# A gated recurrence and highway layer on one core: smaller first units, one shared set of work buffers and a new order of operations

## The chip, the cores and the metric

The kernel runs on one core of a Trainium2 chip. The metric is device time in microseconds; lower is better. Three runs of the kernel before took 207.35, 207.47 and 208.76 us (median 207.47).

## The reference

`x` and `f_logit` are 4 sequences of 6336 tokens with 256 features in fp32. A gated running state goes along each sequence, and a highway layer with two 256x256 matrices follows.

```
sig = 1 / (1 + exp(-f_logit))
f = lower_bound + (1 - lower_bound) * sig;   i = 1 - f
h[t] = f[t] * h[t-1] + i[t] * x[t]           # per sequence and feature, h starts at 0
H = relu(h @ w_h);   T = sigmoid(h @ w_t + b_t)
out = T * H + (1 - T) * h                    # 25344 x 256, fp32
```

## The kernel before, in words

The 25344 tokens are 198 blocks of 128. They are cut into **units** (`parts`): one unit is one tuple, with one or two subtiles of up to 8 blocks, so that (8, 8) is a unit of 2048 tokens. Units are worked in order, since the state runs on from one to the next. The features are two halves of 128 partitions (`h` or `m` = 0, 1). Each step of a unit is one letter in the string `order`, and the program issues the steps exactly as that string lists them; every engine then works its own steps in that order and waits where an input or a buffer isn't ready. The token `s10.0` is the step `s` of unit 10, half 0; the number after a colon names the buffer or the PSUM banks; a `v` at the end puts the step on VectorE (DVE) where it could run on another engine.

The steps, with their engines:

- `l`, `x`: loads of `f_logit` and `x` for one subtile (SP's queue; 1 MB for 8 blocks). `w`: store of a result (SP's queue too).
- `u`: u = sigmoid(-logit), fp16 (ScalarE, ACT).
- `b`, `B`: products bv = u * x, half of a subtile or all of it (GpSimd, POOL; with `v` on DVE).
- `i`, `p`: TensorE (PE) transposes of u and of bv into PSUM. `f`: f = 1 + ncc * u (ACT, with `v` DVE).
- `s`: the scan y = f * y + bv over one half of a unit (DVE). It reads the transposed bv of all the unit's subtiles.
- `z`, `g`: the two matmuls on y. `t`: sigmoid of z (ACT). `d`: max of g and the scaled y (DVE).
- `e`, `E`: the gate d = d * t, for one half or both (POOL, with `v` DVE).
- `o`: matmuls that bring y and d back to token order. `c`: copy out of PSUM (ACT, with `v` DVE).
- `k`: matmuls on zeros, whose result nobody uses.

`WI`, `WH`, `WT`, `dg`, `pc`, `cc` prepare weights and per-feature scalars once. Two rules of the code matter later. The helper `shared` records the last `b` or `e` that DVE did, and makes the next `b` or `e` on POOL wait until that one has ended. And each kind of tile has numbered buffers of its own (`u0`, `bv0`, `f0`, ...), so that a step waits for the last reader of its buffer.

Of the kernel before, what the change touches and what calls it, by code (L numbers as in the profile page):

```python
# [19 lines left out]
def kernel(  # L20
# [454 lines left out]
```

## Time and profile before

| | |
|---|---|
| timed runs | 207.35, 207.47, 208.76 us |
| span of the profiled execution, first to last instruction | 205.8 us (its own device time isn't listed apart; the median of the timed runs lies 1.7 us above the span) |
| instructions | 4646 |
| busy: PE, DVE, ACT, POOL | 194.8, 192.4, 190.7, 173.8 us |
| moved by DMA | 78.67 MB, mean 382 GB/s |
| granted TensorE clock | 0.998 |

A PE that is busy isn't necessarily at its peak, since the ends of matmuls are modelled. DVE and ACT durations are recorded, with successive instructions overlapping a little. In a list by shape, "128x1024" is 128 partitions by 1024 elements of one partition. Idle time is booked to what ended it.

### The profile page before, as it was taken

The page shows a single profiled execution, that of the slowest core. Times are in us where ns is not written, and L with a number is a line of the kernel's source. Part 1 is how long each engine was busy: PE and PEld are TensorE (multiplying, and loading weights), DVE is VectorE, ACT ScalarE, POOL GpSimd, SP SyncE. Part 2 cuts the span into 40 slices and gives each one's busy share as a digit, 9 for nine tenths or more (in the row PEclk, how much of TensorE's full clock was granted, in tenths as well). Part 3 has the DMA queues.
Part 4 walks back from the last instruction along what each step waited for, and adds up shares of the span by engine and source line. Part 5 has one row for each costly group of instructions (what it writes and reads, how often), then busy time and mean ns, then how long its engine had stood idle before and what let it go on. Part 6 is the DMA issues. An engine that isn't in the chain of part 4 may idle for free.

```text
span 205.8 us, 4646 instructions
## 1 busy us (share of the span) xinstructions
PE 194.8 (95%) x1850; PEld 135.7 (66%) x1850; DVE 192.4 (93%) x147; ACT 190.7 (93%) x182; POOL 173.8 (84%) x85
## 2 busy tenths in 40 slices
PE   7989999969989999999999999999999999999992
PEld 2555775746765747757757858657757868777671
DVE  0679999999999999999999999999999999999992
ACT  5197999999999999999999999999999999999992
POOL 3634696999999999979999869999899788999760
PEclk9999999999999999999999999999999999999999
DMA  6999999999999999999999999999999999853766
GB/s 191 375 427 419 417 420 419 414 413 426 416 426 427 414 422 410 432 408 427 426 408 426 427 412 425 419 422 427 414 411 407 334 411 382 344 212 140 277 225 234
DMA packets 16700, 78.67 MB, mean 382 GB/s; under 512 B 1828, under 2 KB 2344, under 8 KB 10792
## 3 DMA queue, kind: packets, MB, share of 16 engines
q1 hardware_dynamic: 16672, 78.39, 93.9%
q8 instruction: 14, 0.23, 0.4%
q14 instruction: 6, 0.05, 0.1%
q10 hardware_dynamic: 8, 0.00, 0.0%
HBM read 52.43 MB, written 25.95 MB: 381 GB/s over the span
## 4 chain that ended last, share of the span: by engine, by line
PE 56%; DVE 24%; ACT 7%; issue 5%; DMA 5%; SPq 0%; DVEq 0%; ACTq 0%
PE psum L344 17%; DVE y L331 15%; PE psum L149 13%; DVE d L374 7%; PE psum L407 7%; PE psum L408 7%; PE psum L322 6%; PE psum L297 5%; ACT f L312 4%; DMA x<-in_x_dram 4%; ACT t L367 2%; DMA l<-in_f_logit_dram 1%; ACT u L273 1%; PE psum L250 1%; ACT o L427 1%
## 5 line engine op out<-in xcount | busy, mean ns | idle before, releaser
L288 POOL TENSOR_TENSOR bv<-u,x 128x1024 bf16<-128x1024 f16 (+2 forms) x39 | 101.4, 2615 | 20.0 <-DVE d L388 10.9
L331 DVE TENSOR_TENSOR_SCAN y<-f,y,psum 128x1024 bf16<-128x1024 f16 (+6 forms) x40 | 103.7, 2612 | 0.5 <-PE psum L407 0.4
L344 PE MATMUL psum<-y,w_sb 128*128 128x512 bf16 (+1 forms) x240 | 79.6, 368 | 4.2 <-ACT f L312 1.9
L388 POOL TENSOR_TENSOR d<-d,t 128x1024 bf16<-128x1024 bf16 (+3 forms) x33 | 71.5, 2180 | 4.6 <-ACT o L427 1.3
L374 DVE SCALAR_TENSOR_TENSOR d<-y,ncc,psum 128x1024 bf16<-128x1024 bf16 (+2 forms) x60 | 62.7, 1084 | 1.1 <-PE psum L344 0.4
L149 PE MATMUL psum<-y,w_sb 128*128 128x512 bf16 x168 | 63.6, 379 | 0.0
L367 ACT ACTIVATE t<-psum,bt 128x1024 bf16<-128x1024 f32 (+2 forms) x60 | 57.4, 988 | 0.9 <-PE psum L344 0.5
L273 ACT ACTIVATE u<-l 128x2048 f16<-128x2048 f32 (+2 forms) x28 | 48.1, 1744 | 6.5 <-DMA l<-in_f_logit_dram 6.5
L312 ACT ACTIVATE f<-psum,ncc 128x1024 f16<-128x1024 f16 (+3 forms) x38 | 50.3, 1344 | 1.2 <-PE psum L297 1.2
L407 PE MATMUL psum<-diag,y 128*128 128x128 f16 x396 | 49.7, 219 | 0.2
L408 PE MATMUL psum<-ident_b,d 128*128 128x128 bf16 x396 | 49.7, 219 | 0.0
L408 PEld LDWEIGHTS <-d 128*128 128x128 bf16 x396 | 43.5, 112 | 3.8 <-DVE d L388 0.4
L427 ACT COPY o<-psum 128x1024 f32<-128x1024 f32 (+1 forms) x46 | 44.2, 997 | 1.6 <-ACT f L312 0.6
L407 PEld LDWEIGHTS <-y 128*128 128x128 bf16 x396 | 43.6, 112 | 2.7
L344 PEld LDWEIGHTS <-w_sb 128*128 128x128 f16 x240 | 23.0, 98 | 20.1 <-issue 0.8
L322 PE MATMUL psum<-ident_f,bv 128*128 128x128 f32 x198 | 29.4, 275 | 0.8 <-ACT f L312 0.7
L149 PEld LDWEIGHTS <-w_sb 128*128 128x128 f16 x168 | 16.4, 97 | 20.2 <-issue 5.9
L297 PE MATMUL psum<-ident_h,u 128*128 128x128 f16 x396 | 28.8, 221 | 0.8 <-DVE y L331 0.4
L297 PEld LDWEIGHTS <-u 128*128 128x128 f16 x396 | 25.1, 99 | 5.7 <-issue 1.2
L322 PEld LDWEIGHTS psum<-ident_f,bv 128*128 128x128 f32 x198 | 22.4, 141 | 5.8 <-ACT f L312 1.4
L388 DVE TENSOR_TENSOR d<-d,t 128x1024 bf16<-128x1024 bf16 (+3 forms) x20 | 11.3, 596 | 0.1
L149 PE MATMUL psum<-zeros 128*128 128x512 bf16 x39 | 10.6, 398 | 0.0
(34 smaller groups left out, 43.1 us busy)
## 6 DMA issues: line engine op xcount, KB each, us to landing
l<-in_f_logit_dram SPq DMA_DIRECT2D x23, 1024.0 KB, 13.6
x<-in_x_dram SPq DMA_DIRECT2D x23, 1024.0 KB, 14.2
out_dram<-o SPq DMA_DIRECT2D x43, 512.0 KB, 8.0
out_dram<-x SPq DMA_DIRECT2D x7, 256.0 KB, 2.0
out_dram<-o SPq DMA_DIRECT2D x6, 256.0 KB, 9.3
l<-in_f_logit_dram SPq DMA_DIRECT2D x2, 512.0 KB, 6.5
x<-in_x_dram SPq DMA_DIRECT2D x2, 512.0 KB, 7.3
l<-in_f_logit_dram SPq DMA_DIRECT2D x3, 256.0 KB, 2.8
```

The source lines that it names most:

```text
L149: return pe.add_instruction(mybir.InstMatmult(name=nc.get_next_instruction_name(), start_tensor_calc=start, stop_tensor_calc=stop, tile_si ...
L288: shared(pin(e.tensor_mul(st[n]["bv", s][:, a:c].rearrange("p k d j -> p k j d"), st[n]["u", s][:, 2 * a:2 * c].rearrange("p (k j) d -> p ...
L297: pin(nc.tensor.transpose(uT[:, j * P:(j + 1) * P], st[n]["u", s][:, j, h * P:(h + 1) * P], ident_h))
L312: pin(nc.scalar.activation(to, of, AF.Identity, scale=ncc[:, h:h + 1], bias=1.0))
L322: pin(nc.tensor.transpose(words[:, k:k + g * (P - 1) + 1:g], pair, ident_f))
L331: pin(nc.vector.tensor_tensor_scan(y[:, c:e], st[n]["f", h][:, c:e], data, 0.0 if fresh else carry[h], op0=ALU.mult, op1=ALU.add))
L344: pin(nc.tensor.matmul(p.part(a, e), w, data, start=ki == 0, stop=ki == NH - 1))
L367: pin(nc.scalar.activation(half(n, q, "t", m), z, AF.Sigmoid, bias=bt[:, m:m + 1]))
L374: pin(nc.vector.scalar_tensor_tensor(half(n, q, "d", m), y, ncc[:, m:m + 1], g, op0=ALU.mult, op1=ALU.max))
L388: shared(pin(e.tensor_mul(d, d, t)), not eng)
L407: pin(nc.tensor.matmul(o, st[n]["y", h][:, whole], diag[:, h], start=True, stop=False))
L408: pin(nc.tensor.matmul(o, half(n, q, "d", h)[:, cols], ident_b, start=False, stop=True))
```

## The change

1. `parts` begins (1,), (1,), (2,), (4,) in place of (2,), (2,), (4,): the same first 8 blocks in four units in place of three, 22 units in all. From the fourth (8,) on everything is cut as before, under a number that is higher by one.
2. `lower_bound` and `moe_b_t` go to tiles of their own and are transposed apart (`pb`, `pc`); `bt` is copied by ACT (`cbv`).
3. `u`, `bv`, `f`, `y`, `t`, `d` and the results `o` take their buffers from one set, `work0` to `work28`; `l` and `x` from another, `large0` to `large9`. For units of at most 1024 tokens the two halves of `f`, and of `y`, lie in one buffer (`halves`).
4. `order` is written anew. Counted over the whole program:

| step and width (elements of one partition) | engine | before | after |
|---|---|---|---|
| products `b` 2048 / 1024 / 512 / 256 | DVE | 0 / 1 / 1 / 0 | 7 / 0 / 0 / 1 |
| products `b` 2048 / 1024 / 512 / 256 | POOL | 12 / 21 / 6 / 0 | 15 / 4 / 2 / 1 |
| gate `e` 2048 / 1024 / 512 / 256 / 128 | DVE | 1 / 11 / 3 / 5 / 0 | 9 / 6 / 2 / 0 / 0 |
| gate `e` 2048 / 1024 / 512 / 256 / 128 | POOL | 5 / 20 / 7 / 1 / 0 | 6 / 9 / 5 / 3 / 2 |
| `f` 1024 / 512 / 256 / 128 | DVE | 1 / 1 / 2 / 0 | 2 / 0 / 0 / 3 |
| copies out 1024 / 512 / 256 | DVE | 2 / 2 / 1 | 2 / 0 / 1 |
| weight scaling 256 | DVE / ACT | 2 / 2 | 4 / 0 |
| matmuls on zeros from `k` | PE | 49 | 23 |

Scans and `d` stay on DVE, with the same total of elements.

The core of the diff, with two lines of the old and the new `order` (the first of each):

```
-    parts = [(2,), (2,), (4,), (8,), (8,), (8,), (8,), (8, 8), ...
+    parts = [(1,), (1,), (2,), (4,), (8,), (8,), (8,), (8,), (8, 8), ...
-k*4:0 l1.0:0 u1.0:0 i1.0.0:0 i1.0.1:1 l0.0:1 x0.0:0 x1.0:1 u0.0:1 b0.0.0:0 pc:2 wh i0.0.0:3 i0.0.1:4 WI k*1:5 cc
+x0.0:0 l2.0:1 pb:0 pc:1 cc l0.0:2 u0.0:0 b0.0.0v:1 l1.0:3 u1.0:2 k*1:6 i0.0.0:7 i1.0.0:6 u2.0:3 i2.0.1:5 f1.0v:4
+    def work(dtype, name, slot):
+        return pool.tile([P, 2 * NB * P], dtype, tag=f"work{slot}", name=name)
+    def large(name, slot):
+        return pool.tile([P, NB, D], FP32, tag=f"large{slot}", name=name)
-    prm = sb([2 * NH, P], FP32, "prm")
-    pin(nc.scalar.dma_start(prm[:NH], lower_bound.rearrange("(h p) -> h p", p=P)))
-    pin(nc.scalar.dma_start(prm[NH:], moe_b_t.rearrange("(h p) -> h p", p=P)))
+    raw_lb = sb([NH, P], FP32, "raw_lb")
+    raw_bt = sb([NH, P], FP32, "raw_bt")
+    pin(nc.scalar.dma_start(raw_lb, lower_bound.rearrange("(h p) -> h p", p=P)))
+    pin(nc.scalar.dma_start(raw_bt, moe_b_t.rearrange("(h p) -> h p", p=P)))
...
-            st[n]["bv", s] = sb([P, NB // 2, D, 2], BF16, "bv", slot)
+            st[n]["bv", s] = work(BF16, "bv", slot)
...
+    def halves(n, name, dtype, h, slot):
+        N = tokens(n)
+        if N > NB * P:
+            st[n][name, h] = work(dtype, name, slot)[:, :N]
+        elif (name, 0) not in st[n]:
+            both = work(dtype, name, slot)
+            st[n][name, 0], st[n][name, 1] = both[:, :N], both[:, N:2 * N]
+        return st[n][name, h]
```

Three places show how the new order stands on the engines.

**The first loads on SP's queue**, before (`l` and `x` of units 1, 0, 2, 3, 4, ...; 512 elements are two blocks, `w_raw` the two weight matrices):

```order
L261 DMA l<-in_f_logit_dram 128x512 x2
L261 DMA x<-in_x_dram 128x512 x2
L208 DMA w_raw<-in_moe_w_h_dram 128x2x256
L261 DMA l<-in_f_logit_dram 128x1024
L205 DMA w_raw<-in_moe_w_t_dram 128x2x256
L261 DMA x<-in_x_dram 128x1024
L261 DMA l<-in_f_logit_dram 128x2048
```

and of the change:

```order
L278 DMA x<-in_x_dram 128x256
L278 DMA l<-in_f_logit_dram 128x512
L278 DMA l<-in_f_logit_dram 128x256 x2
L278 DMA x<-in_x_dram 128x256
L216 DMA w_raw<-in_moe_w_h_dram 128x2x256
L213 DMA w_raw<-in_moe_w_t_dram 128x2x256
L278 DMA x<-in_x_dram 128x512
L278 DMA l<-in_f_logit_dram 128x1024
L278 DMA x<-in_x_dram 128x1024
L278 DMA l<-in_f_logit_dram 128x2048
```

Ahead of the first 1 MB load (128x2048) stand the same bytes as before, 8 blocks of `l`, 8 of `x` and the two matrices, 2.5 MB in all, in smaller pieces and another order.

**DVE in the middle, around the scans of unit 9 before** (`y_1002` and `y_1060` are its two halves, `d_966` the gate of unit 8, the other rows `d` steps of units 7 to 9):

```order
L374 SCALAR_TENSOR_TENSOR d_966<-y_895,ncc_92,psum_61 128x1024
L374 SCALAR_TENSOR_TENSOR d_820<-y_742,ncc_92,psum_61 128x1024
L331 SCALAR_TENSOR_TENSOR y_1002<-f_905,y_895,psum_61 128x2048
L331 SCALAR_TENSOR_TENSOR y_1060<-f_876,y_853,psum_61 128x2048
L388 TENSOR_TENSOR d_966<-d_966,t_1062 128x2048
L374 SCALAR_TENSOR_TENSOR d_1146<-y_853,ncc_92,psum_61 128x1024
```

The same tokens are unit 10 in the change. On DVE (`bv_981` is `B10.0v`, the products of unit 10's first subtile; `y_993` and `y_1048` its scans; `bv_1037` is `B11.1v`; `d_794` and `d_956` the gates `E8.1v` and `E9.1v`):

```order
L310 TENSOR_TENSOR bv_981<-u_784,x_775 128x4x2x256
L364 SCALAR_TENSOR_TENSOR y_993<-f_864,y_895,psum_61 128x2048
L421 TENSOR_TENSOR d_794<-d_794,t_811 128x2048
L310 TENSOR_TENSOR bv_1037<-u_950,x_912 128x4x2x256
L364 SCALAR_TENSOR_TENSOR y_1048<-f_888,y_827,psum_61 128x2048
L421 TENSOR_TENSOR d_956<-d_956,t_999 128x2048
L407 SCALAR_TENSOR_TENSOR d_1123<-y_895,ncc_93,psum_61 128x1024
```

and on POOL beside it (`d_620` is `E7.0`, `bv_983` is `B10.1`, the products of unit 10's second subtile, `d_800` is `E8.0`, `bv_1189` is `B11.0`):

```order
L421 TENSOR_TENSOR d_620<-d_620,t_655 128x2048
L310 TENSOR_TENSOR bv_983<-u_788,x_804 128x4x2x256
L421 TENSOR_TENSOR d_800<-d_800,t_906 128x2048
L310 TENSOR_TENSOR bv_1189<-u_929,x_1035 128x4x2x256
L421 TENSOR_TENSOR d_1123<-d_1123,t_1030 128x1024 x2
```

Products of one unit are now split between the engines: those of the first subtile stand on DVE right ahead of the scan `y_993`, those of the second on POOL behind them, by the rule of `shared`.

**Near the end, DVE of the change** (`y_2302` are scans of unit 18, `y_2399` of 19, `y_2554` of 20; `d_2100` is the gate `E15.0v`, `d_2424` first two `d` steps and then the gate `E18.1v`):

```order
L421 TENSOR_TENSOR d_2100<-d_2100,t_2135 128x2048
L364 SCALAR_TENSOR_TENSOR y_2302<-f_2051,y_2215,psum_61 128x1024
L407 SCALAR_TENSOR_TENSOR d_2361<-y_2215,ncc_93,psum_61 128x1024 x2
L407 SCALAR_TENSOR_TENSOR d_2385<-y_2302,ncc_93,psum_61 128x512
L364 SCALAR_TENSOR_TENSOR y_2399<-f_2290,y_2302,psum_61 128x1024
L407 SCALAR_TENSOR_TENSOR d_2424<-y_2302,ncc_93,psum_61 128x512 x2
L407 SCALAR_TENSOR_TENSOR d_2385<-y_2302,ncc_93,psum_61 128x512
L364 SCALAR_TENSOR_TENSOR y_2399<-f_2290,y_2302,psum_61 128x1024
L421 TENSOR_TENSOR d_2424<-d_2424,t_2456 128x1024
L364 SCALAR_TENSOR_TENSOR y_2554<-f_2466,y_2399,psum_61 128x512 x2
```

and POOL beside it (`B18.0`, `B19.0`, the gates `E16.0` and `E17.0`, `B20.0`, `b21.0.0`):

```order
L310 TENSOR_TENSOR bv_2292<-u_1924,x_1951 128x4x2x256
L310 TENSOR_TENSOR bv_2363<-u_2193,x_2196 128x4x2x256
L421 TENSOR_TENSOR d_2202<-d_2202,t_2224 128x2048
L421 TENSOR_TENSOR d_2361<-d_2361,t_2350 128x2048
L310 TENSOR_TENSOR bv_2397<-u_2374,x_2049 128x2x2x256
L310 TENSOR_TENSOR bv_2472<-u_2431,x_908 128x2x256
```

`bv_2292` stands ahead of DVE's gate `E15.0v`. Between that gate and `E18.1v` POOL now has five whole steps, from `bv_2363` to `bv_2472`; the scans `y_2399` need the first of them, the scans `y_2554` the fourth, `bv_2397`.

More of the change, by code (lines that the diff above doesn't have):

```diff
@@ L317, in do_p @@
             st[n]["bT", h] = Banks(slot, BF16)
+        if units[n][1][s] == 1:
+            pin(nc.tensor.transpose(st[n]["bT", h].one(s)[:, :P], st[n]["bv", s][:, h * P:(h + 1) * P], ident_b))
+            return
         words = st[n]["bT", h].one(s).bitcast(FP32)
```

173 lines of the change are left out of this document (90 added, 83 removed).

## The prediction

> **What bounds the kernel now.** I read the busy times first, then the stages, then the groups of instructions by shape.
>
> ```profile
> PE 194.8 (95%) x1850; PEld 135.7 (66%) x1850; DVE 192.4 (93%) x147; ACT 190.7 (93%) x182; POOL 173.8 (84%) x85
> ```
>
> Four engines are above 80% of a span of 205.8 us, so the average singles out none. The stages do (window, then PE, PEld, DVE, ACT, POOL busy, granted clock, DMA share, GB/s):
>
> ```profile
> 0.00:10.00 10.00, 8.81 (x35) 4.17 (x36) 3.77 (x12) 3.43 (x5) 4.77 (x15) 1.00 0.79 281
> 10.00:25.00 15.00, 14.14 (x109) 8.91 (x107) 12.63 (x19) 13.28 (x19) 6.50 (x4) 1.00 1.01 420
> 25.00:100.00 75.00, 70.55 (x685) 49.81 (x684) 74.30 (x42) 74.06 (x58) 71.60 (x27) 1.00 1.02 419
> 100.00:200.00 100.00, 99.23 (x1005) 71.35 (x1003) 99.70 (x71) 98.06 (x100) 90.90 (x41) 1.00 0.92 368
> 200.00:206.00 6.00, 2.10 (x27) 1.42 (x24) 2.03 (x6) 1.86 (x4) 0.00 (x0) 0.92 0.59 219
> ```
>
> From 25 to 200 us DVE works 174.0 of 175 us. Its idle time is 6.2 + 2.4 = 8.6 us before 25 us and 3.8 us from 200 to the end at 205.8. Is that busy time work, or stretched by waiting? The shapes answer (total busy, mean ns of one, idle before):
>
> ```profile
> L374 DVE SCALAR_TENSOR_TENSOR d<-y,ncc,psum 128x1024 bf16<-128x1024 bf16 x42 | 51.6, 1271 | 0.6 <-issue 0.2
> L288 POOL TENSOR_TENSOR bv<-u,x 128x2048 bf16<-128x2048 f16 x12 | 49.5, 4132 | 3.9 <-DVE d L388 3.9
> L288 POOL TENSOR_TENSOR bv<-u,x 128x1024 bf16<-128x1024 f16 x21 | 45.1, 2161 | 9.7 <-DVE d L388 7.0 <-ACT t L367 2.1 <-ACT u L273 0.6
> L388 POOL TENSOR_TENSOR d<-d,t 128x1024 bf16<-128x1024 bf16 x20 | 42.5, 2137 | 2.3 <-ACT o L427 1.3 <-DVE d L388 1.0
> L331 DVE TENSOR_TENSOR_SCAN y<-f,y,psum 128x1024 bf16<-128x1024 f16 x18 | 41.5, 2331 | 0.4 <-PE psum L407 0.4
> L331 DVE TENSOR_TENSOR_SCAN y<-f,y,psum 128x2048 bf16<-128x2048 f16 x8 | 35.5, 4466 | 0.0
> L388 POOL TENSOR_TENSOR d<-d,t 128x2048 bf16<-128x2048 bf16 x5 | 20.4, 4083 | 0.1
> L388 DVE TENSOR_TENSOR d<-d,t 128x1024 bf16<-128x1024 bf16 x11 | 7.6, 719 | 0.0
> L374 DVE SCALAR_TENSOR_TENSOR d<-y,ncc,psum 128x256 bf16<-128x256 bf16 x6 | 2.6, 470 | 0.0
> L331 DVE TENSOR_TENSOR_SCAN y<-f,y,psum 128x256 bf16<-128x256 f16 x4 | 3.0, 738 | 0.0
> L388 DVE TENSOR_TENSOR d<-d,t 128x256 bf16<-128x256 bf16 x5 | 1.4, 294 | 0.0
> L288 DVE TENSOR_TENSOR bv<-u,x 128x1024 bf16<-128x1024 f16 x1 | 1.3, 1318 | 0.0
> L310 DVE TENSOR_SCALAR f<-psum,ncc 128x1024 f16<-128x1024 f16 x1 | 1.3, 1271 | 0.0
> L388 DVE TENSOR_TENSOR d<-d,t 128x512 bf16<-128x512 bf16 x3 | 1.3, 448 | 0.1
> L388 DVE TENSOR_TENSOR d<-d,t 128x2048 bf16<-128x2048 bf16 x1 | 1.2, 1200 | 0.0
> L236 DVE TENSOR_SCALAR w_sb<-w_raw,cc 128x256 f16<-128x256 f32 x2 | 0.8, 444 | 0.0
> L288 DVE TENSOR_TENSOR bv<-u,x 128x512 bf16<-128x512 f16 x1 | 0.7, 745 | 1.5 <-DMA x<-in_x_dram 1.5
> L425 DVE COPY o<-psum 128x512 f32<-128x512 f32 x1 | 0.7, 667 | 0.0
> ```
>
> A scan of 2048 elements takes 4466 ns and one of 1024 takes 2331, a constant 2.08 ns per element plus 0.2 us; one of 256 (738) lies on the same line. There is no room for hidden waits. **DVE's own work paces the kernel** from 25 us on, ACT is 1.9 us behind it, and POOL has slack.
>
> **The work that moves to DVE.** The step from 512 to 1024 elements of a product costs 1318 - 745 = 573 ns, so 2048 elements cost 1318 + 2 x 573 = 2464 ns.
>
> - Products: 7 x 2.46 = 17.2 us more, one of 256 (745 - 287 = 458 ns) 0.5 more, less 1.32 and 0.75: +15.6.
> - Gates: now 9 x 1.200 + 6 x 0.719 + 2 x 0.448 = 16.0; before 1.2 + 11 x 0.719 + 3 x 0.448 + 5 x 0.294 = 11.9: +4.1.
> - Small edits together: one more `f` of 1024 (1.27) and three of 128 (0.34 each, extrapolated) for 2.0 us of old ones, +0.3; two copies of 512 fewer, -1.3; weight scaling, +0.9; 8 scans and 8 `d` at the start in place of 6 each (six of 256 become four of 256 and four of 128, by the rows of 256 about 0.47 and 0.34 for 128), +0.9; the copy of `bt` gone, -0.1. Sum +0.7.
>
> That is 20.4 us in 7 more instructions. Successive instructions overlap: 42 `d` of 1271 ns are 53.4 us by themselves and 51.6 together, some 0.05 us each, so 0.4 is taken off. DVE's work becomes 192.4 + 20.0 = **212.4 us**, more than the whole span before. The bounds: if a product of 2048 went by the 1.04 ns per element of `d` (1271 ns per 1024) it would take 2.38 us, 0.6 less in all; the extrapolations may be off by 0.2 each, so 211 to 214.
>
> POOL loses 17 x 2.16 + 4 x 1.17 of products and 11 x 2.14 + 2 x 1.16 of gates, and gains 3 x 4.13 + 4.08 and some 2.5 of small ones: about 48 us less, 126 in all. On ACT 192 us remain (two weight scalings fewer, more short instructions). Neither shortens anything, since DVE has no idle time to give back. The 26 zero matmuls that go would be some 10 us of PE's time (398 ns each):
>
> ```profile
> L149 PE MATMUL psum<-zeros 128*128 128x512 bf16 x39 | 10.6, 398 | 0.0
> ...
> 5.43 0.63 PE L297 MATMUL psum<-ident_h,u 128*128 128x128 f16 x4
> ...
> 11.74 0.39 PE L297 MATMUL psum<-ident_h,u 128*128 128x128 f16 x4
> ```
>
> I cost them at nothing: DVE's queue covers them. Where it doesn't, at the start, four transposes at 5.4 us took 0.63 and at 11.7 us, behind a row of zero matmuls, 0.39; if PE stays slow for ten such groups, that is up to 2.4 us, and if PE is freed earlier it is a gain of less.
>
> **The start.** What do the first units gain?
>
> ```profile
> 11.42 0.74 DVE L288 TENSOR_TENSOR bv<-u,x 128x512 bf16<-128x512 f16 x1 [1.48 <-DMA x<-in_x_dram]
> ...
> 13.85 1.91 ACT L273 ACTIVATE u<-l 128x2048 f16<-128x2048 f32 x1 [0.17 <-DMA l<-in_f_logit_dram]
> ...
> 18.90 1.91 ACT L273 ACTIVATE u<-l 128x2048 f16<-128x2048 f32 x1 [0.47 <-DMA l<-in_f_logit_dram]
> ```
>
> The first full load lands at 13.85 us and the second `l` at 18.9, with 2 MB in 5.05 us (DMA share 1.01): the loads themselves set the pace. The bytes ahead of them are the same 2.5 MB in the change, so the smaller pieces only rearrange the time before. In the change's DVE order the products `B5.0v` come ahead of the scans of unit 4, and they need `x` of unit 5, the fourth 1 MB load: 18.9 + 2.5 = 21.4 us. Then follow B5.0v 2.4, two scans 4.5, `f` 1.2, two `d` 2.4, `B6.0v` 2.4: the end of `B6.0v` is at 34.3 us. Up to there DVE's order holds 27.2 us of work (the scans of units 0 to 4, their `d`, three products of 2048 and the preparations, by the rows above). So 7.1 us are idle at the start, where 8.6 were: **a gain of 1.5 us.** The bounds are 0 (another wait before `B5.0v`) and 3.
>
> **The end.**
>
> ```profile
> 201.12 0.48 DVE L388 TENSOR_TENSOR d<-d,t 128x256 bf16<-128x256 bf16 x2
> 201.93 0.42 DVE L425 COPY x<-psum 128x256 f32<-128x256 f32 x1 [0.33 <-PE psum L408]
> ```
>
> From the last gate's end (201.6) to the end of the span are 4.2 us with one copy of 0.4 on DVE; the last units are cut as before, and I keep 3.8 us of idle time. Without any new wait the span would be 212.4 + 7.1 + 3.8 = 223.3.
>
> **The new waits.** Which DVE steps need something that POOL starts only after a DVE step just ahead? POOL's time is 4.13 us for 2048 products, twice what DVE needs, and `shared` doesn't let it start earlier.
>
> ```profile
> 92.50 0.44 PE psum L322 x4
> ```
>
> - After `B10.0v` DVE's next row is the scan `y_993`, which needs `B10.1` too. POOL may begin that only when `B10.0v` has ended: 4.1 us, then two rounds of transposes (0.44 each) and about 0.1 of signalling: **5.1 us idle**, with gate, products and scan of the other half queued behind it on DVE. In the kernel before, that scan had a `d` or another scan ahead of it and all products on POOL.
> - After `E15.0v` DVE holds three scans of 1024 (2.26 each by their overlapping times), two `d` of 1024 (1.2) and four of 512, 11.8 us in all, and POOL 4.1 + 4.1 + 4.1 + 2.2 + 1.2 = 15.7 of which the first four, 14.5, plus a transpose must end before the scans `y_2554`: **3 us idle.**
> - After `B17.0v` the scan needs that very product transposed: 0.44 + 0.2 = 0.6.
> - The port. A gate on DVE and a product on POOL seem to exclude each other:
>
> ```profile
> 162.74 6.24 POOL L288 TENSOR_TENSOR bv<-u,x 128x1024 bf16<-128x1024 f16 x2
> ...
> 168.53 0.99 DVE L388 TENSOR_TENSOR d<-d,t 128x1024 bf16<-128x1024 bf16 x1
> ...
> 171.82 0.68 DVE L388 TENSOR_TENSOR d<-d,t 128x1024 bf16<-128x1024 bf16 x1
> ```
>
> The gate at 168.53, with POOL busy until 168.98, took 0.99 us; the one at 171.82, just after POOL's next step, 0.68. So one that meets POOL waits. In the change `e4.0.1v` stands 4.5 us of DVE work behind `B6.0v`, while POOL has 2.1 + 4.1; `E13.0v` stands 5.6 behind `E12.1v`, with 2.1 + 4.1 + 2.1 on POOL. I take 1 us for each, and 1.5 for all the rest, between nothing and 4.
>
> The sum of waits is 5.1 + 3.0 + 0.6 + 2.0 + 1.5 = 12.2; the bounds are 8 (the first three less a microsecond) and 24 (the other places twice or thrice as long). The span comes to 223.3 + 12.2 = 235.5, and with 1.7 around it the time is **237 us**.
>
> [...]
>
> **The rivals.**
>
> *Only the work counts.* POOL may be late or early in another way, and the waits vanish into each other: 223.3 + 1.7 = 225 us. For it speaks that before, DVE lost almost nothing between 25 and 200 us; against it the order, in which nothing stands on DVE between `B10.0v` and its scan. Chance 0.10.
>
> *The port costs much more.* 25 steps of DVE (17 gates, 8 products) now contend. With POOL busy 126 of 235 us and steps of up to 4.1 us, a chance meeting costs 0.54 x 2.1 = 1.1 us; 24 of them 26 us instead of the 3.5 taken: 260 us. Against it: DVE is last, so POOL has usually finished its share before the next shared step. Likewise a shared work buffer that is released late would show as waits of DVE or ACT. Chance 0.08.
>
> *Not slower: POOL paced the kernel.* If the steps that POOL hands on had set DVE's pace, 48 us less there would free DVE, and the next bound is ACT: 192 us of work, with the 15.1 us that ACT idles now less the 1.5 of the start, 205.6, so 207 us; with less idle time below 205. The point that decides is whether DVE's 192.4 us hold 20 us of waiting for POOL.
>
> ```profile
> POOL bv L288 <- DVE d L388: 10.9, 7, 3.9
> ```
>
> Here POOL waits for DVE, 10.9 us in 7 times, and the scans' even 2.08 ns per element leave no such waiting: chance 0.04. [...]
>
> That the change doesn't do what it says is excluded by the counts of its instructions on each engine.
>
> **How the numbers follow.** Forecast 0.78, work alone 0.10, port 0.08, not slower 0.04. The predicted time is the forecast's, 237. Its own range, from waits of 8 and work of 211 to waits of 24 and work of 214, less or more 1 at the start, is 230 to 251. To take in the rival of work alone, the range goes down to 225; up it ends at 250, and leaves out the port's 260 and the fourth case, about 0.14 with the forecast's upper tail. Within 1% is what a measurement here can't tell from no change. Faster by more: 0.02; within 1%: 0.02; slower by more: 0.96.
>
> **What would show it.** DVE's busy time near 212 us and the highest of all, POOL's near 126; DVE products of 2048 at 2.4 to 2.5 us; an idle stretch of about 5 us on DVE ahead of the first half's scan of unit 10, ended by a PE transpose, and one of about 3 near the end; the end of `B6.0v` at 34 us; ACT, PE and DMA with idle time in the middle. I am wrong if DVE isn't the fullest engine, if its products take under 2 us, or if PE or ACT end most of its idle time.

## The result and the profile after

The change takes **249.83 us** (median of five runs, 248.01 to 250.5), the kernel before 207.47 in the same five rounds: a ratio over the runs of 1.2016, with a 95% interval of 1.197 to 1.2063. The profiled execution took 248.01 us, the least of the five, with a span of 246.2. Among the experiments one execution, of 309.67 us at a mean granted clock of 0.662, lies far outside all others and is left out.

The busy times of the whole span, from the page of the changed kernel:

```profile
PE 199.4 (81%) x1835; PEld 136.6 (55%) x1835; DVE 217.4 (88%) x154; ACT 192.6 (78%) x188; POOL 128.0 (52%) x60
```

DVE has gone from 192.4 to 217.4 us and POOL from 173.8 to 128.0, while ACT still does its 191 to 193 us. DVE is alone at the top now, and yet at 88% it is emptier than before, at 93%. The stages show where (window, then PE, PEld, DVE, ACT, POOL busy, granted clock, DMA share, GB/s):

```profile
0.00:10.00 10.00, 4.89 (x20) 1.83 (x20) 4.71 (x16) 4.16 (x9) 3.10 (x14) 0.93 0.72 216
10.00:25.00 15.00, 13.57 (x98) 9.07 (x98) 10.02 (x15) 11.35 (x16) 8.35 (x9) 0.82 1.02 423
25.00:75.00 50.00, 37.49 (x331) 24.41 (x330) 49.87 (x27) 37.98 (x31) 26.62 (x8) 0.93 0.97 398
75.00:100.00 25.00, 16.76 (x141) 11.48 (x140) 18.48 (x10) 16.70 (x13) 10.44 (x4) 0.88 0.78 293
100.00:200.00 100.00, 92.00 (x896) 64.57 (x894) 98.81 (x56) 90.84 (x77) 56.60 (x19) 0.98 0.83 310
200.00:247.00 47.00, 34.72 (x354) 25.27 (x354) 35.54 (x33) 31.56 (x45) 22.94 (x9) 0.96 0.65 256
```

DVE's idle time is 10.3 us before 25 us, 6.5 between 75 and 100, 1.3 in the two full stages together, and 10.7 from 200 us to the end of the span at 246.2. The DMA share, 1.02 from 25 to 100 us and 0.92 from 100 to 200 before, is 0.78 to 0.97 here from 25 to 200 us. What DVE does more of, by shape (total busy, mean ns, idle before):

```profile
L310 DVE TENSOR_TENSOR bv<-u,x 128x2048 bf16<-128x2048 f16 x7 | 17.4, 2489 | 1.7 <-ACT u L290 1.7
L421 DVE TENSOR_TENSOR d<-d,t 128x2048 bf16<-128x2048 bf16 x9 | 10.8, 1213 | 0.0
L421 DVE TENSOR_TENSOR d<-d,t 128x1024 bf16<-128x1024 bf16 x6 | 7.8, 1314 | 0.0
```

The gates of 1024 have a mean of 1314 ns where they had 719: one of the six was held up for long, as shown below. The longest waits of DVE (what it waited for, us in total, times, longest):

```profile
DVE y L364 <- PE psum L356: 8.1, 3, 6.5
DVE ncc L228 <- PE psum L220: 3.3, 1, 3.3
DVE d L407 <- PE psum L156: 2.8, 2, 2.4
DVE y L364 <- PE psum L350: 2.2, 1, 2.2
```

**At the start** a further wait, for ACT, holds up the products `B5.0v` on DVE's timeline (start, duration, engine, line, operation, count, idle before and what ended it):

```profile
24.95 2.56 DVE L310 TENSOR_TENSOR bv<-u,x 128x2048 bf16<-128x2048 f16 x1 [1.68 <-ACT u L290]
```

**Unit 10's first scan** has the longest wait. The timelines of DVE, POOL and PE:

```profile
91.05 2.42 DVE L310 TENSOR_TENSOR bv<-u,x 128x2048 bf16<-128x2048 f16 x1
99.93 4.48 DVE L364 TENSOR_TENSOR_SCAN y<-f,y,psum 128x2048 bf16<-128x2048 f16 x1 [6.45 <-PE psum L356]
...
93.73 4.08 POOL L310 TENSOR_TENSOR bv<-u,x 128x2048 bf16<-128x2048 f16 x1 [14.56 <-DVE bv L310]
...
97.87 1.97 PE L356 MATMUL psum<-ident_f,bv 128*128 128x128 f32 x8 [7.71 <-POOL bv L310]
```

DVE's product ends at 93.47; POOL, which had nothing to do for 14.56 us, begins its own 0.26 us later and takes 4.08; then eight transposes take 1.97 us. All of this stands between two neighbouring instructions of DVE.

**The held gate** of unit 4 and the end, on the same timelines:

```profile
42.52 4.06 DVE L421 TENSOR_TENSOR d<-d,t 128x1024 bf16<-128x1024 bf16 x1
...
41.95 4.09 POOL L310 TENSOR_TENSOR bv<-u,x 128x2048 bf16<-128x2048 f16 x1 [1.52 <-ACT u L290]
...
204.59 2.35 DVE L364 TENSOR_TENSOR_SCAN y<-f,y,psum 128x1024 bf16<-128x1024 f16 x1 [1.21 <-PE psum L356]
208.95 2.35 DVE L364 TENSOR_TENSOR_SCAN y<-f,y,psum 128x1024 bf16<-128x1024 f16 x1 [2.01 <-ACT f L344]
...
213.76 1.20 DVE L421 TENSOR_TENSOR d<-d,t 128x2048 bf16<-128x2048 bf16 x1
...
219.62 3.26 DVE L407 SCALAR_TENSOR_TENSOR d<-y,ncc,psum 128x1024 bf16<-128x1024 bf16 x3 [2.40 <-PE psum L156]
...
215.02 0.25 PE L441 MATMUL psum<-ident_b,d 128*128 128x128 bf16 x1 [3.67 <-DVE d L421]
```

The gate at 42.52 doesn't end before POOL's product does, at 46.04. At the end DVE loses 1.21 + 2.01 + 0.20 + 2.40 us around unit 17. The last of these is a ring: PE stops in unit 15's `o` for 3.67 us, until DVE's gate `E15.0v` at 213.76 has ended; behind it in PE's queue stand the matmuls `z` and `g` of unit 17, for which DVE's `d` of unit 17 then waits.

### The profile page after: what moved, and what is told of

It is laid out like the page before. It is cut to its first block, busy times and chain, and to the rows that moved or that the text cites. A ratio compares the mean times of both kernels' runs of the same rounds, so it can differ in the third digit from the quotient of the medians.

```text
span 246.2 us, 4565 instructions
## 1 busy us (share of the span) xinstructions
PE 199.4 (81%) x1835; PEld 136.6 (55%) x1835; DVE 217.4 (88%) x154; ACT 192.6 (78%) x188; POOL 128.0 (52%) x60
## 4 chain that ended last, share of the span: by engine, by line
PE 38%; DVE 38%; issue 11%; POOL 5%; DMA 2%; ACT 2%; SPq 1%; DVEq 0%; POOLq 0%; ACTq 0%
DVE y L364 21%; PE psum L377 12%; DVE d L407 9%; PE psum L156 9%; DVE bv L310 5%; PE psum L356 5%; PE psum L441 4%; PE psum L440 4%; POOL bv L310 4%; PE psum L319 3%; DMA x<-in_x_dram 2%; DVE d L421 2%; POOL d L421 2%; ACT t L400 1%; SPq L278 1%
## 5 line engine op out<-in xcount | busy, mean ns | idle before, releaser
L364 DVE TENSOR_TENSOR_SCAN y<-f,y,psum 128x1024 bf16<-128x1024 f16 (+7 forms) x42 | 104.9, 2514 | 12.7 <-PE psum L356 8.1
L310 POOL TENSOR_TENSOR bv<-u,x 128x2048 bf16<-128x2048 f16 (+2 forms) x21 | 72.6, 3464 | 68.1 <-DMA out_dram<-o 16.1
L377 PE MATMUL psum<-y,w_sb 128*128 128x512 bf16 (+2 forms) x248 | 83.4, 381 | 13.1 <-DVE y L364 8.8
L400 ACT ACTIVATE t<-psum,bt 128x1024 bf16<-128x1024 f32 (+3 forms) x62 | 57.0, 954 | 32.5 <-PE psum L156 29.8
L421 POOL TENSOR_TENSOR d<-d,t 128x1024 bf16<-128x1024 bf16 (+4 forms) x25 | 52.9, 2129 | 37.4 <-DVE bv L310 28.1
L407 DVE SCALAR_TENSOR_TENSOR d<-y,ncc,psum 128x1024 bf16<-128x1024 bf16 (+3 forms) x62 | 63.1, 1060 | 5.0 <-PE psum L156 2.8
L456 ACT COPY o<-psum 128x1024 f32<-128x1024 f32 (+2 forms) x55 | 48.8, 910 | 8.5 <-issue 4.6
L290 ACT ACTIVATE u<-l 128x2048 f16<-128x2048 f32 (+3 forms) x29 | 48.2, 1685 | 5.7 <-DMA l<-in_f_logit_dram 5.7
L344 ACT ACTIVATE f<-psum,ncc 128x1024 f16<-128x1024 f16 (+4 forms) x39 | 49.9, 1307 | 2.8 <-PE psum L319 2.8
L156 PEld LDWEIGHTS <-w_sb 128*128 128x128 f16 x168 | 17.2, 102 | 24.8 <-issue 11.8
L421 DVE TENSOR_TENSOR d<-d,t 128x2048 bf16<-128x2048 bf16 (+2 forms) x17 | 19.5, 1154 | 0.2
L310 DVE TENSOR_TENSOR bv<-u,x 128x2048 bf16<-128x2048 f16 x7 | 17.4, 2489 | 1.7 <-ACT u L290 1.7
## 6 DMA issues: line engine op xcount, KB each, us to landing
l<-in_f_logit_dram SPq DMA_DIRECT2D x2, 512.0 KB, 10.7
```

The lines of the kernel that those rows point to most:

```text
L156: return pe.add_instruction(mybir.InstMatmult(name=nc.get_next_instruction_name(), start_tensor_calc=start, stop_tensor_calc=stop, tile_si ...
L310: shared(pin(e.tensor_mul(st[n]["bv", s][:, a:c].rearrange("p k d j -> p k j d"), st[n]["u", s][:, 2 * a:2 * c].rearrange("p (k j) d -> p ...
L344: pin(nc.scalar.activation(to, of, AF.Identity, scale=ncc[:, h:h + 1], bias=1.0))
L364: pin(nc.vector.tensor_tensor_scan(y[:, c:e], st[n]["f", h][:, c:e], data, 0.0 if fresh else carry[h], op0=ALU.mult, op1=ALU.add))
L377: pin(nc.tensor.matmul(p.part(a, e), w, data, start=ki == 0, stop=ki == NH - 1))
L400: pin(nc.scalar.activation(half(n, q, "t", m), z, AF.Sigmoid, bias=bt[:, m:m + 1]))
```

## The experiments

Each kernel differs from the change, or from the kernel before, only in the tokens shown (fragments of `order`). Times are medians, beside 207.1 to 207.6 us for the kernel before in the same rounds.

### Products back on GpSimd

```
-B4.0v:25 B5.0v:1 B6.0v:4 B10.0v:11 B11.1v:18 B14.1v:26 B17.0v:25
+B4.0:25 B5.0:1 B6.0:4 B10.0:11 B11.1:18 B14.1:26 B17.0:25
```

> The change with its seven products of 2048 elements back on POOL (B4.0, B5.0, B6.0, B10.0, B11.1, B14.1, B17.0); all else as in the change. Theory (DVE's work plus its waits set the time): DVE loses 7 x 2.42 = 17 us of busy time, down to about 200; the 6.5 us wait ahead of unit 10's first scan goes, since POOL may now do both products of unit 10 early; the time falls from 249.8 to 224 to 232 us. Rival (the new order and the half-speed stretches of TensorE set the time): less than 8 us are gained, 242 or more. Rival (POOL was relieved for a reason): POOL rises to 157 us and its slower products come late for the scans; slower than 249.8.

Measured: **227.32 us**, ratio 1.0953 (1.0889 to 1.1018). The page:

```profile
PE 195.5 (87%) x1835; PEld 136.7 (61%) x1835; DVE 198.0 (88%) x147; ACT 192.3 (86%) x188; POOL 156.7 (70%) x67
```

This is within the theory's range, and the wait ahead of unit 10's first scan is gone: from 25 to 150 us DVE idles 0.8 us in all. DVE's busy time falls by 19.4 us, its idle time from 28.8 to 25.9. Seven instructions carry 22.5 of the 42 us. What is left lies at the start (10.5 us idle before 25 us) and near the end: between 173 and 200 us DVE idles 10.2 us, in much the same waits as above.

### Seven products moved in the kernel before

```
-B7.0:2 B8.0:0 B9.0:2 B11.0:1 B13.0:0 B14.0:2 B16.0:2
+B7.0v:2 B8.0v:0 B9.0v:2 B11.0v:1 B13.0v:0 B14.0v:2 B16.0v:2
```

> The kernel before with seven of its twelve whole-subtile products moved from POOL to DVE (B7.0, B8.0, B9.0, B11.0, B13.0, B14.0, B16.0), order and buffers untouched: one part of the change alone. Theory (DVE paces): DVE gains 7 x 2.42 = 17 us and the time rises to 224 plus the new waits at the port, 224 to 235 us. Rival (POOL paced the kernel, DVE had hidden slack): 200 to 212 us.

Measured: **241.64 us**, ratio 1.1654 (1.1595 to 1.1713): 34.5 us for seven products, and 6.6 us above the theory's upper end. DVE by shape:

```profile
L288 DVE TENSOR_TENSOR bv<-u,x 128x2048 bf16<-128x2048 f16 x7 | 20.2, 2880 | 0.4 <-ACT u L273 0.4
```

and the waits of DVE and of POOL:

```profile
DVE y L331 <- PE psum L322: 13.2, 7, 6.5
...
POOL bv L288 <- DVE bv L288: 17.9, 2, 15.8
POOL bv L288 <- DVE d L388: 15.2, 6, 7.2
```

DVE's busy time rises by 21.2 us to 213.6 and its idle time by 13.2. The one long wait for transposes is here seven waits, 13.2 us in all, and POOL, with 24 us less to do, stands idle for DVE's products and gates for 33.1 us in these two rows. That work on POOL paces is refuted.

### Gates back on GpSimd

```
-E5.0v E8.1v E9.1v E11.1v E12.1v E13.0v E14.0v E14.1v E15.0v
+E5.0 E8.1 E9.1 E11.1 E12.1 E13.0 E14.0 E14.1 E15.0
```

> The change with its nine gates of 2048 elements on GpSimd in place of VectorE; all else, the products too, as in the change. Theory (VectorE's own work paces, wherever it comes from): 9 gates of 1213 ns less overlap, about 10.3 us, leave VectorE, whose busy time comes to about 207 us, and the time falls from 249.8 to 236 to 243 us; GpSimd's busy time rises from 128 to about 165 us. Rival (GpSimd then hands on its products late, twice 4 us in a row, and VectorE waits for them): 246 us or more, with more idle time ahead of scans.

Measured: 248.3 us, the median of three executions, ratio 1.1995 (1.1951 to 1.204). The theory missed: nothing clear of the scatter was gained. The kernel was run once more for its profile.

> The same kernel again, nine gates of 2048 back on GpSimd, for its profile, since its time of 248.8 us was the change's own although about 10 us of work left VectorE. Theory (GpSimd's 4.1 us steps, now 9 more of them, are handed on late: a gate on GpSimd holds TensorE's queue until it ends, and VectorE waits for the matmuls behind): VectorE busy about 207 us, with 10 us more idle time than in the change, ended by TensorE, in the stages where the gates stood. Rival (the two engines exclude each other, and VectorE's instructions are longer): VectorE's busy time stays at 213 us or more. Time 247 to 250 us.

Measured: 247.81 us. The page:

```profile
PE 199.4 (81%) x1835; PEld 136.9 (56%) x1835; DVE 210.9 (86%) x145; ACT 192.5 (78%) x188; POOL 163.6 (67%) x69
```

DVE by shape, one row:

```profile
L421 DVE TENSOR_TENSOR d<-d,t 128x1024 bf16<-128x1024 bf16 x6 | 9.2, 1541 | 0.0
```

and one row of its waits:

```profile
DVE d L407 <- ACT o L456: 5.5, 3, 3.6
```

Nine gates of 1213 ns left DVE, but its busy time fell by 6.5 us only: the gates of 1024 went from 1314 to 1541 ns and the products from 2489 to 2684, beside a POOL that was busy for 163.6 us in place of 128.0. And idle time rose by 6.3 us to 35.1: `d` now waits 5.5 us for ACT's copies out, which follow PE's `o`, which gets the gated values later than in the change, by an estimated 4.08 - 1.21 = 2.9 us. So both the theory and its rival held in part. In this order, with the seven products on DVE, a gate on DVE is worth about as much to those who wait for it as it costs.

### Both moves undone

```
-B4.0v:25 B5.0v:1 B6.0v:4 B10.0v:11 B11.1v:18 B14.1v:26 B17.0v:25
+B4.0:25 B5.0:1 B6.0:4 B10.0:11 B11.1:18 B14.1:26 B17.0:25
-E5.0v E8.1v E9.1v E11.1v E12.1v E13.0v E14.0v E14.1v E15.0v
+E5.0 E8.1 E9.1 E11.1 E12.1 E13.0 E14.0 E14.1 E15.0
```

> The change with both moves undone, seven whole products and nine gates of 2048 on GpSimd; the smaller first units, the shared buffers and the new order stay. Theory (work plus waits): the 227.3 us of the run with only the products back, less about 10.3 us of gates, gives 217 us (212 to 222), VectorE busy near 188 us and GpSimd near 193; what is left over 207 us is the order's waits and the head. Rival A (the order and the buffers cost most, not the moves): 225 us or more. Rival B (nothing but the moves costs time): 205 to 210 us.

Measured: **224.37 us**, ratio 1.0821 (1.0787 to 1.0854), between the theory and rival A.

```profile
PE 193.4 (87%) x1835; PEld 135.1 (61%) x1835; DVE 191.2 (86%) x138; ACT 192.1 (86%) x188; POOL 191.6 (86%) x76
```

DVE has less work than in the kernel before (191.2 against 192.4), but POOL has 17.8 us more, mostly since that kernel had kept one gate of 2048, eleven of 1024 and five of 256 on DVE, and the new order only six of 1024. DVE idles 31.4 us. With the products back, moving the gates back too gained 3.0 us (224.4 after 227.3), not the 10 of the theory; with the products on DVE it had gained nothing clear. And with both moves undone the kernel is still 16.9 us slower than the kernel before. No run separates what of that belongs to the smaller first units, the shared buffers and the new order.

### Gates alone moved in the kernel before

```
-E5.0 E6.0 E7.1 E11.0 E15.0
+E5.0v E6.0v E7.1v E11.0v E15.0v
```

> The kernel before with its five gates of 2048 elements that ran on GpSimd (units 5, 6, 7, 11 and 15) put on VectorE, each at its place in the order; all products stay on GpSimd. Moving nine gates back to GpSimd left the change's time as it was, so the price of a gate on VectorE is open. Theory A (VectorE's own work paces, and each gate costs its 1.2 us): 6.0 us more, 212 to 216 us, VectorE busy near 198.5. Theory B (a gate on VectorE costs next to nothing, since TensorE gets the gated values 2.9 us sooner and the relief of GpSimd gives the time back): 206 to 210 us. Theory C (besides its 1.2 us each gate waits for a product that GpSimd has under way): over 216 us, with VectorE's gates of 2048 well above 1.2 us.

Measured: **224.13 us**, ratio 1.0818 (1.0786 to 1.0849): by its number theory C, but for another reason. DVE by shape:

```profile
L388 DVE TENSOR_TENSOR d<-d,t 128x2048 bf16<-128x2048 bf16 x6 | 8.0, 1347 | 0.0
```

The waits of DVE and of POOL:

```profile
DVE d L374 <- PE psum L149: 8.7, 5, 4.2
POOL bv L288 <- DVE d L388: 30.7, 7, 12.3
```

And the timelines of DVE, POOL and PE around the first of the five gates:

```profile
60.90 1.20 DVE L388 TENSOR_TENSOR d<-d,t 128x2048 bf16<-128x2048 bf16 x1
66.32 1.28 DVE L374 SCALAR_TENSOR_TENSOR d<-y,ncc,psum 128x1024 bf16<-128x1024 bf16 x1 [4.21 <-PE psum L149]
...
62.36 13.36 POOL L288 TENSOR_TENSOR bv<-u,x 128x2048 bf16<-128x2048 f16 x4 [12.27 <-DVE d L388]
...
62.16 0.30 PE L408 MATMUL psum<-ident_b,d 128*128 128x128 bf16 x1 [4.43 <-DVE d L388]
```

Gates held up beside POOL's work are a small part: only one was long (2.04 us), and the mean is 1347 ns. Of 16.8 us, 7.8 are DVE's busy time and 8.6 its idle time. The gate `E5.0v` had to wait in DVE's queue behind scans until 60.90, where POOL had begun it at 50.34 in the kernel before; POOL, whose next products may not start before DVE's gate has ended (by the helper `shared`), was idle for 12.27 us, and PE stood for 4.43 us in `o` of unit 5 with the matmuls behind it that DVE's next `d` needs.

### The order of unit 10's products

```
-B10.0v:11 B10.1:23
+B10.1:23 B10.0v:11
```

> The change with one token moved: POOL's products of unit 10's second subtile (B10.1) stand ahead of DVE's products of its first subtile (B10.0v), so that the rule of shared no longer makes POOL wait for DVE there. Theory (that wait is paid in full because DVE is the pacing engine): the idle stretch of 6.5 us ahead of the scan shrinks to about 1 (one transpose round on TensorE), and the time falls by 5 to 6 us, to 244. Rival (the time is given back by a later wait for ScalarE or TensorE): 248 or more.

Measured: **243.98 us**, ratio 1.1766 (1.1683 to 1.1849), 5.9 us less, as expected. The scan:

```profile
93.54 4.48 DVE L364 TENSOR_TENSOR_SCAN y<-f,y,psum 128x2048 bf16<-128x2048 f16 x1 [1.26 <-PE psum L356]
```

The wait is 1.26 us where it was 6.45. The order of two neighbouring tokens was worth 2.3% of the time by the medians. The profiled spans differ by 2.7 us only (246.2 and 243.5): DVE idles 4.3 us from 100 to 200 us, where it was 1.2, so in this execution part of the gain was given back.

### Zero matmuls for the clock

```
-p2.0.0:5
+k*8:1 p2.0.0:5
-p10.1.0:67
+k*16:0 p10.1.0:67
-p17.0.1:7
+k*10:2 p17.0.1:7
```

> The change with 34 matmuls on zeros put into three stretches where TensorE idles: 8 ahead of the transposes of unit 2's products, 16 ahead of those of unit 10's second subtile, 10 ahead of those of unit 17. Theory (an idle TensorE drops to half clock, and DVE waits for its slow transposes): the eight transposes ahead of unit 10's scan take 0.9 us in place of 1.97, those of unit 17 half as long; the mean granted clock rises from 0.945 towards 0.96, and the time falls by 1.5 to 3 us. Rival (the clock doesn't matter, DVE waits for products and not for TensorE): within 1 us of 249.8.

Measured: 246.03 us, ratio 1.1861 (1.1793 to 1.193), so 3.8 us less by the medians, and each of the four executions took less than each of the change's five. But for the cause this remains **inconclusive**. At unit 10 the sixteen matmuls ran as soon as they could, from 89.75 to 93.15 us, and PE then waited 4.29 us again:

```profile
97.44 1.97 PE L356 MATMUL psum<-ident_f,bv 128*128 128x128 f32 x8 [4.29 <-POOL bv L310]
```

The transposes were as slow as without them. At unit 17 the ten matmuls did what they were meant to do: four transposes took 0.65 us, where they had taken 1.11 in the change, and DVE's waits ahead of the two scans were 0.75 and 1.00 us in place of 1.21 and 2.01. DVE's next wait took it back, 4.04 us where it had been 2.40:

```profile
219.27 3.26 DVE L407 SCALAR_TENSOR_TENSOR d<-y,ncc,psum 128x1024 bf16<-128x1024 bf16 x3 [4.04 <-PE psum L156]
```

In between PE stands 3.67 us for the gate `E15.0v`, in both profiles; behind that its granted clock is 0.50 here (214 to 216 us) and 1.00 in the change (215 to 217 us). The two profiles differ by 1.2 us of span, and by 1.8 at the start alone (8.5 us idle before 25 us, against 10.3), where other kernels with an unchanged start have 8.4 to 9.5. So neither of the two places explains the 3.8 us, and what a clock kept up throughout would be worth isn't settled.

### A product behind the gate that it held up

```
-B7.0:15 p6.0.0:5 e4.0.1v
+p6.0.0:5 e4.0.1v B7.0:15
```

> The change with GpSimd's products of unit 7 handed out behind VectorE's gate of unit 4's second half, in place of ahead of it; no work is added or moved to another engine. In the profile of the change that gate took 4.06 us with GpSimd's product running, other gates of its width 0.67 to 0.72. Theory (the two exclude each other, and the gate waited for the product's end): the gate takes 0.7 us, and the time falls by 3.4 us to about 246.4 us (245.5 to 247.5). Rival (the products of unit 7, now some 1.5 us later, are waited for in turn, or other work was late too): 248.5 to 250.5 us.

Measured: 248.83 us, ratio 1.2019 (1.1971 to 1.2067): the rival.

```profile
41.41 0.67 DVE L421 TENSOR_TENSOR d<-d,t 128x1024 bf16<-128x1024 bf16 x1
...
45.18 1.28 DVE L407 SCALAR_TENSOR_TENSOR d<-y,ncc,psum 128x1024 bf16<-128x1024 bf16 x1 [0.85 <-PE psum L156]
48.56 2.35 DVE L364 TENSOR_TENSOR_SCAN y<-f,y,psum 128x1024 bf16<-128x1024 f16 x1 [2.10 <-PE psum L356]
```

The gate takes 0.67 us, so the hold-up was real, 3.4 us of it. But DVE, earlier by that much and by 1.1 us from the start, now waits 0.85 + 2.10 us for PE. The products of unit 7, which the rival names, aren't waited for. PE had stood still for 3.81 us ahead of the matmuls of unit 5, and its granted clock is 0.50 from 41.5 to 47 us; in the change it is 0.51 from 42.6 to 45.6 us and 1.00 from 46.9 to 50. The same sixteen transposes, here and in the change:

```profile
44.93 1.91 PE L319 MATMUL psum<-ident_h,u 128*128 128x128 f16 x16
...
46.04 1.07 PE L319 MATMUL psum<-ident_h,u 128*128 128x128 f16 x16
```

The transposes of unit 6 that the second waiting scan needs stand behind them, and PE comes to them at 47.85 us, in the change at 47.81. What had been booked as busy time had covered this wait for PE.

### The gate of unit 15

```
-d16.0.1 B17.0v:25
+d16.0.1 E15.0v B17.0v:25
-s18.1:4 E15.0v s18.0
+s18.1:4 s18.0
```

> The change with VectorE's gate of unit 15 ahead of the products of unit 17, where it stood between the scans of unit 18; nothing else moves. In the profile of the change TensorE waits 3.67 us for that gate with the matmuls of unit 17 queued behind it, VectorE then 2.40 us for those matmuls ahead of its d steps of unit 17. Theory: that wait goes, 2.4 us, and with the matmuls also GpSimd's products of unit 19 come earlier: 246 to 248 us, no idle time of over 1 us ahead of d of unit 17. Rival (the next wait takes its place): 249 to 250.5 us.

Measured: **245.52 us**, ratio 1.1846 (1.18 to 1.1892), 4.3 us less, a little more than the theory's bound. DVE's wait ahead of `d` of unit 17 is gone:

```profile
211.98 2.35 DVE L364 TENSOR_TENSOR_SCAN y<-f,y,psum 128x1024 bf16<-128x1024 f16 x1 [3.07 <-ACT f L344]
...
219.20 3.11 DVE L407 SCALAR_TENSOR_TENSOR d<-y,ncc,psum 128x1024 bf16<-128x1024 bf16 x3
```

So the ring through PE's `o` was the cause of that wait. The wait for `f` has grown from 2.01 to 3.07, so part was given back, and the profiled spans differ by 1.5 us only (246.2 and 244.7). The profiles don't show where the rest of the 4.3 us comes from.

### Five places mended

```
-t3.0.1:24 t3.0.0
+l5.0:2 u5.0:27 t3.0.1:24 t3.0.0
...
-l5.0:2 u5.0:27 c0.0.0:28
+c0.0.0:28
-B7.0:15 p6.0.0:5 e4.0.1v
+p6.0.0:5 e4.0.1v B7.0:15
-B10.0v:11 B10.1:23
+B10.1:23 B10.0v:11
-B17.0v:25 p17.0.1:7 s17.1:3 w13.0.1 w13.1.0 w13.0.0 z16.0.0:23 t16.0.0:15 w11.1.0 o14.0.1:01 i17.0.0:6 f17.0 p17.0.0:4
+E15.0v B17.0v:25 w13.0.1 w13.1.0 w13.0.0 z16.0.0:23 t16.0.0:15 w11.1.0 o14.0.1:01 i17.0.0:6 f17.0 p17.0.1:7 s17.1:3 p17.0.0:4
-s18.1:4 E15.0v s18.0
+s18.1:4 s18.0
```

> The change with five places of its order mended and every step on the engine where the change has it: GpSimd's product of unit 10 ahead of VectorE's, its product of unit 7 behind the gate of unit 4, the gate of unit 15 ahead of the products of unit 17, TensorE's transposes of these products behind the matmuls of unit 16 and the transposes for f of unit 17, and the sigmoid of unit 5 ahead of two of unit 3. Theory (the waits are local, and the work on VectorE stays): 249.8 less 5.9, 1.0, 4.3, 2 to 3 for f of unit 17 and 1.2 at the start gives 235 us (232 to 238), VectorE busy 213 to 215 us with 18 to 22 us idle. Rival (a wait that is removed comes back at the next place): 240 us or more.

Measured: **238.77 us**, ratio 1.1516 (1.1449 to 1.1584), 11.1 us less: 0.8 us above the theory's range.

```profile
PE 201.0 (85%) x1835; PEld 138.5 (59%) x1835; DVE 214.3 (91%) x154; ACT 192.5 (82%) x188; POOL 128.8 (55%) x60
```

and one row of DVE's timeline:

```profile
23.50 2.45 DVE L310 TENSOR_TENSOR bv<-u,x 128x2048 bf16<-128x2048 f16 x1 [0.36 <-ACT u L290]
```

DVE is busy for 214.3 us and idle for 21.1 of a span of 235.4, as the theory has it, and `f` of unit 17 isn't waited for. The wait for the sigmoid of unit 5 is down from 1.68 to 0.36. Its span is still 29.6 us longer than that of the kernel before: 21.9 us more of DVE's busy time and 7.7 more of idle time, of which a new order alone could remove only the second and some hold-ups.

### Products back, and the end mended

```
-B4.0v:25 B5.0v:1 B6.0v:4 B10.0v:11 B11.1v:18 B14.1v:26 B17.0v:25
+B4.0:25 B5.0:1 B6.0:4 B10.0:11 B11.1:18 B14.1:26 B17.0:25
...
-B17.0:25 p17.0.1:7 s17.1:3 w13.0.1 w13.1.0 w13.0.0 z16.0.0:23 t16.0.0:15 w11.1.0 o14.0.1:01 i17.0.0:6 f17.0 p17.0.0:4
+E15.0v B17.0:25 w13.0.1 w13.1.0 w13.0.0 z16.0.0:23 t16.0.0:15 w11.1.0 o14.0.1:01 i17.0.0:6 f17.0 p17.0.1:7 s17.1:3 p17.0.0:4
-s18.1:4 E15.0v s18.0
+s18.1:4 s18.0
```

(and, as above, `u5.0` ahead of two steps of unit 3.)

> The change with its seven whole products on GpSimd, and with three places mended: the gate of unit 15 ahead of the products of unit 17, their transposes behind the matmuls of unit 16 and the transposes for f of unit 17, and the sigmoid of unit 5 ahead of two of unit 3. With the products alone moved back the time was 227.3 us, of which VectorE idled 10.2 us from 173 to 200 us. Theory (those waits come from the order around unit 17, not from the products): 217 to 221 us, VectorE busy 198 us, at most 3 us idle between 150 us and the last 10. Rival (the waits are GpSimd's products of units 17 to 20, which come late): 224 to 228 us.

Measured: **221.95 us**, ratio 1.0688 (1.0645 to 1.0731), just outside the theory's range.

```profile
184.78 4.59 DVE L364 TENSOR_TENSOR_SCAN y<-f,y,psum 128x1024 bf16<-128x1024 f16 x2 [5.42 <-PE psum L356]
...
179.49 12.23 POOL L310 TENSOR_TENSOR bv<-u,x 128x2048 bf16<-128x2048 f16 x3 [15.30 <-DMA out_dram<-o]
```

Of 10.2 us of waits 7.2 remain, in a new place. POOL's products of unit 17 begin at 179.49, where they began at 175.08 with the products alone moved back, and DVE waits 5.42 us for them. The edit itself seems to have done it: DVE's gate of unit 15 now stands ahead of them, and it ended at 179.36. The trace names a store of results instead, and the two weren't told apart. No experiment led to a version as fast as the kernel before.

## Why the prediction was right or wrong, point by point

The predicted 237 us was 12.8 us under the measured median, and the range of 225 to 250 held it at its very end. That it did is partly luck: two of the five executions took over 250 us, and the errors of all five terms below go the same way. The spans, predicted and profiled, 235.5 and 246.2, differ by 10.7 us, which come from five terms:

| term | predicted | measured | more |
|---|---|---|---|
| DVE's work without hold-ups | 212.4 | 213.0 | 0.6 |
| DVE's steps held up beside POOL's | 2.0 | 4.4 | 2.4 |
| idle at the start | 7.1 | 10.3 | 3.2 |
| new waits in the middle and near the end | 10.2 | 14.5 | 4.3 |
| idle at the end, after the last long wait | 3.8 | 4.0 | 0.2 |

- **DVE bounds, and its work grows by 20 us: right.** 217.4 us less the hold-ups of 3.4 (the gate of unit 4) and 1.0 (the `dg` steps and the gate `E18.1v`, longer by 0.6 and 0.4 while POOL was at work) is 213.0. Products took 2489 ns (2464 predicted) and gates 1213 (1200); POOL came to 128.0 us (126). That the products are the largest part is shown by moving them back (22.5 us). Three small figures of the sum don't follow from its own rows, and none moves the forecast by more than 0.3 us: the old `f` steps are 0.75 + 2 x 0.48 = 1.7 us, not 2.0; 26 of the 39 zero matmuls that took 10.6 us are 7 us, not 10; and 4.13 us is 1.7 times DVE's 2.46, not twice.
- **A moved step is priced at its duration on DVE: wrong as a rule.** In the kernel before five gates cost 16.8 us for 6.0 us of work, and seven products 34.5 us for 17.2; in the change nine gates cost nothing net. My sum had the waits as a list of places; it had no term for a step's place in the queue. The price is the duration, and with it how long POOL and PE wait for the step's place in DVE's queue, less what they gain by having it earlier.
- **Unit 10: right in place and kind, 6.45 us against 5.1.** The transposes took 1.97 us, not two rounds of 0.44. The handovers, put at 0.1 without a row, took 0.26 to POOL, 0.06 to PE and 0.09 to DVE. The prediction had seen slow transposes only at the start and had put PE's side at nothing elsewhere; the last section shows what PE's clock did here.
- **The 3 us near the end: the wrong place.** I had put them at unit 20's scans. These waited for nothing of that kind; 5.8 us were lost at units 17 and 18 instead. I had followed only what POOL must finish after `E15.0v`, not PE, which stood in `o` for that very gate (moving it removed the wait of 2.40 us, and 4.3 us of the time). The 0.6 after `B17.0v` was 1.21.
- **The port: the place of one right, its size and meaning wrong.** The gate of unit 4 was held for 3.4 us, not 1, and `E13.0v` not at all. Yet taking the hold-up away returned nothing clear of the scatter, since a wait for PE, with 0.50 of its clock granted, stood behind it. No run shows a port as such, or what a meeting costs in general; the runs show the steps that grew longer beside POOL's.
- **The start: wrong.** `B5.0v` began at 24.95, not at 21.4, where the prediction has its load land: the step that failed is that it needs only `x`. Its `u` stood in ACT's queue behind `f` of unit 4 and `t` of unit 3, and the `B6.0v` that I had ending at 34.3 ended at 38.1. This wait of 1.68 us is half of what was missed; the other half lies earlier, since DVE's steps ahead of `B5.0v` had ended only at 23.27. The parameters reached DVE 1.9 us earlier than before, with no gain. Part of the size is chance: in other kernels with the same start `B5.0v` began between 23.5 and 25.3 us.
- **A criterion that was badly chosen.** I had written that I'd be wrong if PE ended most of DVE's idle time. It did (8.1 + 3.3 + 2.8 + 2.2 us and smaller ones), though the longest of these waits is POOL's product, seen through the transposes behind it.
- **The rivals.** Work alone (225 us) is refuted: the new waits are in the profile, 14.5 us of them, and with five places mended 238.8 us remain. That POOL paced the kernel is refuted by the products moved in the kernel before, which made it slower by 34.5 us while POOL went idle. A costly port (260 us) isn't borne out: the 26 us were an estimate that let all DVE's gates and products contend, and 4.4 us were measured.

## What to carry to other kernels

Before a step moves to the fullest engine, price it three times: its duration there, what its old engine and the matmul queue will wait for while it stands in the new queue, and what they gain if it is done sooner. Splitting one scan's inputs between two engines that the program makes take turns (here by `shared`) puts both shares in a row (up to 6.5 us here), unless the slower engine's share is handed out first. And an order that has been fitted to one placement of steps should be judged with that placement: nine gates on DVE cost the change nothing, 3.0 us once its products were back on POOL, and five cost the old order 16.8 us.

## What the hardware showed that wasn't expected

**In a wait of 7.71 us TensorE's granted clock fell to 0.50, and the transposes behind it took 1.97 us in place of 1.04.** Stretches around unit 10 (columns as in the stages above; the granted clock is the third number from the end):

```profile
90.00:93.00 3.00, 0.15 (x3) 0.00 (x0) 3.00 (x2) 1.85 (x2) 0.00 (x0) 1.00 0.95 371
93.00:96.00 3.00, 0.00 (x0) 0.00 (x0) 0.47 (x1) 0.00 (x0) 2.27 (x1) 0.64 1.00 421
96.00:99.00 3.00, 1.13 (x6) 1.14 (x7) 0.00 (x0) 0.00 (x0) 3.00 (x2) 0.50 1.08 401
```

and the same eight transposes elsewhere, on PE's timeline:

```profile
210.25 1.04 PE L356 MATMUL psum<-ident_f,bv 128*128 128x128 f32 x8
```

PE had been idle since 90.2 us. The granted clock was 1.00 in the stretch from 90 us, 0.64 in that from 93 and 0.50 in that from 96, and eight fp32 transposes took 1.97 us, where the same eight took 1.04 at 210.25, with 1.00 granted from 209 to 212. In the kernel before the clock's mean was 0.998. The same was seen at the start: PE waited 3.72 us until 11.33, and 0.50 was granted from 10 to 15 us in the profile of the change, but 1.00 from 10 to 25 us in that of the kernel with the gate of unit 15 moved, which may be why kernels with this start differ by nearly 2 us there. After waits of about that length the traces show both: 0.51 from 42.6 to 45.6 us in the change after one of 3.33 us, and after one of 3.67 us for the same gate 1.00 in the change and 0.50 in the kernel with more zero matmuls.

**A hold-up of DVE beside POOL was recorded as busy time.** The gate that took 0.67 us with POOL's product behind it appears as one of 4.06 with no idle time ahead of it, so only its shape's mean (1314 against 719 ns) gives it away. It ended 0.54 us after POOL's product.
